# Another order of a pair's score tiles, and the first pair's last tile directly in front of the sums

## The chip, the cores and the metric

The kernel runs on one core of a Trainium2 chip. The metric is the device time of the whole launch in microseconds, smaller is better. The engines are named as the profile names them: PE (TensorE, matmuls) and PEld (its weight loads), DVE (VectorE), ACT (ScalarE), POOL (GpSimd), SP (the queue that issues most DMAs).

## The reference

The input is `x` of 2048 tokens by 448 features. It is normalised (layer norm), and the output is `x` plus attention of the normalised input plus a gated feed-forward layer (FFN) of it:

```python
x = A_x
xn = _layernorm(x, axis=-1)
return x + _A_ref(xn, ...) + _B_ref(xn, ...)
# attention: 16 heads of 28, four segments s of L = 512 tokens
logits = jnp.einsum("bhqd,bhkd->bhqk", qs, ks) * scale + mask      # causal, within the segment
a_dot = jnp.einsum("bhqk,bhkd->bhqd", _softmax(logits, axis=-1), vs)
o = g * a_mem + (1.0 - g) * a_dot          # a_mem: recall from a running memory of earlier segments
# FFN
h = _sigmoid(g) * u                        # g, u: xn times w_gate, w_up (448 x 1792)
return jnp.einsum("bsf,fd->bsd", h, w_down)
```

## The kernel before

A first part (up to about 160 us) normalises, makes queries, keys and values, and does the memory recall. The second part, in which the change lies, runs the FFN and the attention interleaved. The orders of PE and SP are those of the code (`MANUAL`); the orders of ACT, DVE and POOL are chosen by the framework's scheduler, which puts the instructions of both parts into one queue for each engine.

The FFN is a generator. For each of 4 token blocks and each pair of hidden strips it issues runs of 11 matmuls of 512 columns into a bank `pgu` (L247) and, later, runs of six matmuls of 448 columns into `pd` (L173), which DVE adds to `acc` (L174). Between, ACT and DVE make the gated value (`sg`, `hh`, L255 to L259).

The attention is a second generator, of 16 units (counted from 0 here: four segments by four groups of four heads), two pairs of heads each. A unit has 14 slots, and `SLOT` says what stands in each: 0 or 1 is the next step of that pair, 2 the sums of the unit before. The outer loop at the end of the kernel takes a slot from the attention whenever the FFN has gone far enough, so that the slots are spread evenly between the FFN's runs.

A pair's first five steps are its score tiles (`scores`). One tile fills one bank `st` (tag "s", two banks in turn) with keys on the partitions: a head's first key block against 512 queries; its second and fourth blocks, 384 and 128 columns; or both heads' third block, 256 columns twice. Each tile is copied by ACT to `w` (L616 or L619), POOL masks the diagonal blocks (L627), and DVE takes the maximum (L629 over 1024 columns of a head when both of its own tiles are there, L633 over the 512 of the shared tile). A bank can be written again when ACT has copied the tile before the last. After the fifth tile a pair has five more steps (`PARTS`, one at each later slot): a chain of small maxima on DVE and copies on POOL (L643 to L653), a transpose that spreads the maximum (`mb`, L656), and three steps of a subtraction on DVE (L666) and an exponential on ACT (L667). With its last score tile a pair also hands SP the loads of `qk` for the same pair of the next unit (L595); slot 7 hands it the load of `vv` (L679).

The sums (`finish`) are 32 matmul records of 32-column weights, four side by side, from the exponentials and the values into `pa` (L687); DVE then transposes, scales and transposes back (L690, L135, L136, L693).

Of the kernel before, what the change touches and what calls it, by code (L numbers as in the profile page):

```python
# [16 lines left out]
P = 128  # L17
# [5 lines left out]
L = 512  # L23
# [12 lines left out]
LEAD, TAIL = 15, 53  # L36


SLOT = (0, 0, 0, None, 0, 0, None, 2, 1, 1, 1, None, 1, 1)

PARTS = 5

# [1 line left out]
HW = 1280  # L44
# [17 lines left out]
def kernel(  # L62
# [11 lines left out]
    V, A, G, T = nc.vector, nc.scalar, nc.gpsimd, nc.tensor  # L74
# [40 lines left out]
    def bank(name, tag):  # L115
        return ps.tile([P, L], F32, name=name, tag=tag, bufs=banks[tag])
# [159 lines left out]
    with tc.tile_pool(name="front", bufs=2) as sb, tc.manual_schedule(engines=FRONT):  # L276
# [227 lines left out]
        for b in range(NB):  # L504
# [24 lines left out]
            for k, c in enumerate((3, 4, 5, 6, 0, 1, 2) if last else range(7)):  # L529
# [34 lines left out]
                n = k - 1 if b == 0 else k + 1  # L564
# [18 lines left out]
    class Pair:  # L583
# [19 lines left out]
        def scores(self):  # L603

            self.w = sb.tile([P, 2 * HW], F32, name="w", bufs=3)
            w3 = self.w.rearrange("p (h n) -> p h n", h=2)
            mx = sb.tile([P, 80], F32, name="mx", bufs=2)
            for n in range(5):
                st = bank("st", "s")
                for h, kb in (((n // 2, 0),), ((n // 2, 1), (n // 2, 3)))[n % 2] if n < 4 else ((0, 2), (1, 2)):  # L610
                    at = KB[kb] % L + (256 * h if kb == 2 else 0)
                    T.matmul(st[:, at:at + L - kb * P], self.qk[:KS, 1, h, kb * P:(kb + 1) * P],  # L612
                             self.qk[:KS, 0, h, kb * P:], start=True, stop=True)
                if n < 4:
                    w = self.w[:, HW * (n // 2) + L * (n % 2):][:, :L]
                    A.activation(w, st, AF.Copy)  # L616
                else:
                    w = w3[:, :, 2 * L:]
                    A.activation(w, st.rearrange("p (h n) -> p h n", h=2), AF.Copy)  # L619

                if n % 2 == 0 and n < 4:
                    d = w[:, :P]
                    pattern = [[1, P]]
                else:
                    d = w.rearrange("p (a n) -> p a n", n=P)[:, 0:4:3, :] if n < 4 else w[:, :, :P]
                    pattern = [[0, 2], [1, P]]
                G.affine_select(d, d, pattern=pattern, base=0, channel_multiplier=-1, compare_op=ALU.is_ge, fill=MASK)  # L627
                if n in (1, 3):
                    V.tensor_reduce(mx[:, 16 * (n - 1):16 * (n + 1)],  # L629
                                    w3[:, n // 2, :2 * L].rearrange("p (b n) -> p b n", n=32),  # L630
                                    axis=mybir.AxisListType.X, op=ALU.max, apply_transpose=True)
                if n == 4:
                    V.tensor_reduce(mx[:, 64:80].rearrange("p (h b) -> p h b", h=2),  # L633
                                    w.rearrange("p h (b n) -> p h b n", n=32),
                                    axis=mybir.AxisListType.X, op=ALU.max, apply_transpose=True)
                yield
            yield from self.weights(mx)
# [60 lines left out]
    units = [Unit(u, pairs[2 * u:2 * u + 2]) for u in range(NB * NG)]  # L698

    def attention():  # L700
        for n in range(2):
            pairs[n].load()
        units[0].load_values()
        yield
        run, behind, fin = {}, [], None
        for u in range(len(units) + 1):
            for n in range(2):
                run[n] = pairs[2 * u + n].scores() if u < len(units) else iter(())
            for k, which in enumerate(SLOT):
                if u == len(units):  # L710

                    if k > 9:
                        break
                    which = ((None,) * 8 + (2, None))[k]
                if behind:
                    next(behind.pop(0))
                if fin:
                    next(fin)
                    fin = None
                if which is not None and which < 2 and u < len(units):  # L720
                    next(run[which])
                    n = 2 * u + which + 2
                    if which not in SLOT[k + 1:]:
                        behind += [run[which]] * PARTS
                        if n < len(pairs):
                            pairs[n].load()
                        else:
                            load_sums(n - len(pairs))
                if which == 2 and u > 0:
                    fin = units[u - 1].finish()  # L730
                    next(fin)
                    if u < len(units):
                        units[u].load_values()
                yield
# [3 lines left out]
    def load_sums(b):  # L738

        if b < 2:  # L740
            sums[b] = sb.tile([P, HG, L], F32, name="sums", tag="qk2", bufs=2)
        else:
            sums[b] = sums[b - 2]
        o3 = od[b].rearrange("(h c) n -> h c n", c=32)
        for m in range(8):
            a, c = m % 2, 4 * min(m, 6)
            nc.sync.dma_start(sums[b][64 * a:64 * a + 64, m // 2, :], o3[:, c:c + 4, :])
# [32 lines left out]

    N_OUT = 1 + NB * NT * 3 + 12
    steps = attention()
    n_att = len(units) * len(SLOT) + 10
    done = 0
    with tc.manual_schedule(engines=MANUAL):
        next(steps)
        k = sum(FILLS) + 6
# [46 lines left out]
```

## Time and profile before

| | us |
|---|---|
| median of 3 runs (lowest, highest) | 687.41 (687.20, 687.65) |
| the profiled execution | 687.43 |
| its span, first to last instruction | 685.7 |
| PE busy in the span | 679.6 |
| DVE busy | 566.7 |
| ACT busy | 341.6 |
| POOL busy | 147.6 |

The granted TensorE clock is 1.000 over the span. The profile's rows name an engine, a line of the code, an operation and what it writes and reads; behind the bar stand busy time, the mean of one in ns, and the idle time of the engine just before with what ended it. In the order of time, "x11" merges instructions of one line that follow each other, with the shape of the first of them.

### The profile page before, as it was taken

To read this page: it belongs to the slowest core of one execution; us is meant where nothing else is said; L and a number is where in the kernel's file an instruction comes from. 1 tells how busy PE (TensorE), PEld (TensorE's weight loads), DVE (VectorE), ACT (ScalarE), POOL (GpSimd) and SP (SyncE) were. 2 spreads that over 40 slices of the span, in tenths; PEclk is the share of its full clock that TensorE was granted. 3 is DMA by queue.
4 is the path that set the end of the run, shared out by engine and by line. 5 is a ranking of instruction groups with operands and counts; after the bars stand their busy time and mean duration, and the time that the engine had idled before them with its cause. 6 is when DMAs were issued, how large, how long until landed. Compare 5 with 4: busy or idle time off the path is not lost.

```text
span 685.7 us, 10450 instructions
## 1 busy us (share of the span) xinstructions
PE 679.6 (99%) x3594; PEld 565.5 (82%) x3594; DVE 566.7 (83%) x994; ACT 341.6 (50%) x563; POOL 147.6 (22%) x349
## 2 busy tenths in 40 slices
PE   8999999999999999999999999999999999999997
PEld 7898878778878787887878778787887878778897
DVE  6765695767789998988998889988998899889863
ACT  4837555343554455544556446455643465446220
POOL 3500010101223232222232222232321323212000
PEclk9999999999999999999999999999999999999999
DMA  7446556697242333243324243324342423423342
GB/s 268 179 153 233 204 207 244 246 337 179 71 95 78 94 87 86 58 127 83 85 58 112 58 127 70 99 57 117 82 102 69 97 56 86 95 78 91 93 155 107
DMA packets 45796, 84.37 MB, mean 123 GB/s; under 512 B 6320, under 2 KB 20400, under 8 KB 45232
## 3 DMA queue, kind: packets, MB, share of 16 engines
q1 hardware_dynamic: 42736, 76.37, 36.4%
q0 software_dynamic: 3008, 7.34, 5.2%
q8 instruction: 28, 0.46, 0.3%
q14 instruction: 24, 0.20, 0.1%
HBM read 51.05 MB, written 32.64 MB: 122 GB/s over the span
## 4 chain that ended last, share of the span: by engine, by line
PE 97%; DMA 1%; DVE 1%; SPq 0%; issue 0%; ACT 0%; ACTq 0%
PE pgu L247 41%; PE pd L173 20%; PE pp L355 10%; PE st L612 6%; PE pa L687 5%; PE po L771 5%; PE pv L335 5%; PE pmm L383 2%; PE n L401 2%; DMA acc<-in_x 1%; PE pt L95 1%; PE pk L375 1%; DMA vv<-vd 0%; DVE stats L294 0%; DVE acc L775 0%
## 5 line engine op out<-in xcount | busy, mean ns | idle before, releaser
L247 PE MATMUL pgu<-xs,wgu 128*128 128x512 f32 x1232 | 303.6, 393 | 0.0
L247 PEld LDWEIGHTS pgu<-xs,wgu 128*128 128x128 f32 x1232 | 228.2, 188 | 46.9 <-issue 2.4
L173 PE MATMUL pd<-wdn,hh 128*128 128x448 f32 x672 | 155.9, 367 | 0.0
L173 PEld LDWEIGHTS pd<-wdn,hh 128*128 128x128 f32 x672 | 122.4, 188 | 12.0 <-issue 0.8
L627 POOL TENSOR_SCALAR_AFFINE_SELECT w<-w 128x256 f32<-128x256 f32 (+1 forms) x160 | 80.3, 505 | 240.9 <-ACT w L616 192.4
L667 ACT ACTIVATE w<-w 128x1024 f32<-128x1024 f32 (+1 forms) x96 | 87.4, 916 | 88.4 <-DVE w L666 87.9
L666 DVE TENSOR_TENSOR w<-w,mb 128x1024 f32<-128x1024 f32 (+1 forms) x96 | 98.6, 1035 | 0.2
L616 ACT ACTIVATE w<-st 128x512 f32<-128x512 f32 x128 | 74.7, 591 | 43.2 <-PE st L612 42.9
L629 DVE TRANSPOSE_TENSOR_REDUCE mx<-w 128x32 f32<-128x1024 f32 x64 | 78.8, 1231 | 14.8 <-POOL w L627 14.7
L355 PE MATMUL pp<-xs,wqk 128*128 128x512 f32 x308 | 77.7, 401 | 0.0
L174 DVE TENSOR_TENSOR acc<-pd,acc 128x448 f32<-128x448 f32 x112 | 67.2, 600 | 1.1 <-PE pd L173 1.1
L355 PEld LDWEIGHTS pp<-xs,wqk 128*128 128x128 f32 x308 | 56.8, 188 | 13.4 <-issue 2.4
L612 PE MATMUL st<-qk 84*128 84x128 f32 (+3 forms) x256 | 62.3, 313 | 0.1
L258 ACT ACTIVATE hh<-sg 128x512 fp32r<-128x512 f32 x56 | 35.2, 628 | 53.4 <-DVE sg L256 42.2
L612 PEld LDWEIGHTS st<-qk 84*128 84x128 f32 x256 | 47.7, 189 | 7.5 <-ACT w L616 0.7
L255 ACT ACTIVATE sg<-pgu 128x512 f32<-128x512 f32 x56 | 33.1, 592 | 36.2 <-PE pgu L247 36.2
L656 DVE STREAM_TRANSPOSE mb<-top 128x1024 f32<-128x1024 f32 x32 | 39.7, 1242 | 12.6 <-POOL top L653 12.3
L362 DVE TENSOR_TENSOR qk<-pp,qk 128x512 fp32r<-128x512 f32 x28 | 19.3, 689 | 29.8 <-ACT e L360 23.7
L259 DVE SCALAR_TENSOR_TENSOR hh<-sg,hh 128x512 fp32r<-128x512 f32 x56 | 38.9, 694 | 2.8 <-ACT hh L258 2.4
L335 PE MATMUL pv<-wv,xs 128*128 128x448 f32 x176 | 39.6, 376 | 0.4 <-DVE xs L102 0.3
L256 DVE SCALAR_TENSOR_TENSOR sg<-sg,pgu 128x512 f32<-128x512 f32 x56 | 37.3, 667 | 1.7 <-PE pgu L247 1.5
L687 PE MATMUL pa<-w,vv 128*32 128x128 f32 (+3 forms) x512 | 37.9, 436 | 0.0
(100 smaller groups left out, 639.5 us busy)
## 6 DMA issues: line engine op xcount, KB each, us to landing
qk<-qd SPq DMA_DIRECT2D x192, 112.0 KB
qd<-qk SPq DMA_DIRECT2D x28, 512.0 KB
raw<-in_w_ffn SPq DMA_DIRECT2D x14, 512.0 KB
vd<-vst SPq DMA_DIRECT2D x4, 1024.0 KB
vv<-vd SPq DMA_DIRECT2D x16, 256.0 KB
od<-w POOLq DMA_DIRECT2D x16, 256.0 KB, 3.9
sums<-od SPq DMA_DIRECT2D x32, 128.0 KB
out<-acc SPq DMA_DIRECT2D x16, 224.0 KB
```

The costliest lines, as they stand in the source:

```text
L173: T.matmul(pd[:, :D], l, r, start=n == 0, stop=n == len(mms) - 1)
L174: V.tensor_add(acc[b][:, t, :], pd[:, :D], acc[b][:, t, :])
L247: T.matmul(dst, wgu[f][:, w, side * P:(side + 1) * P], xs[b][:, a, :], start=n == 0, stop=n == len(TERMS) - 1)
L335: T.matmul(pv[:, :D], xs[b][:, a, t * P:(t + 1) * P], wv[w], start=n == 0, stop=n == len(TERMS) - 1)
L355: T.matmul(pp, wqk[c][:, w, :], xs[b][:, a, :], start=n == 0, stop=n == len(TERMS) - 1)
L612: T.matmul(st[:, at:at + L - kb * P], self.qk[:KS, 1, h, kb * P:(kb + 1) * P], self.qk[:KS, 0, h, kb * P:], start=True, stop=True)
L616: A.activation(w, st, AF.Copy)
L627: G.affine_select(d, d, pattern=pattern, base=0, channel_multiplier=-1, compare_op=ALU.is_ge, fill=MASK)
L629: V.tensor_reduce(mx[:, 16 * (n - 1):16 * (n + 1)], w3[:, n // 2, :2 * L].rearrange("p (b n) -> p b n", n=32), axis=mybir.AxisListType.X, ...
L666: V.tensor_sub(w, w, m)
L667: A.activation(w, w, AF.Exp, scale=SCALE)
L687: T.matmul(pa[32 * j:32 * j + 32, kb * P:], self.vv[:, kb, 32 * j:32 * j + 32], self.pairs[j // 2].block(j % 2, kb), start=kb == 0, stop=k ...
```

## The change

The order of a pair's five tiles changes. Before: first head 512, first head 384 and 128, second head 512, second head 384 and 128, both heads 256. After: first head 512, second head 512, both heads 256, first head 384 and 128, second head 384 and 128. The reductions move with the tiles: the one of 512 columns comes third instead of last.

The slots change for the first pair: its tiles stood in slots 0, 1, 2, 4, 5 and now stand in 0, 1, 3, 5, 7. A slot can now hold two things, and slot 7 holds the first pair's last tile and, behind it, the sums. Everything that follows a pair's last tile (the five later steps and the load of `qk`) moves from slot 5 to slot 7 with it. The second pair stays in slots 8, 9, 10, 12, 13.

```diff
-SLOT = (0, 0, 0, None, 0, 0, None, 2, 1, 1, 1, None, 1, 1)
+SLOT = ((0,), (0,), (), (0,), (), (0,), (), (0, 2), (1,), (1,), (1,), (), (1,), (1,))
...
             for n in range(5):
                 st = bank("st", "s")
-                for h, kb in (((n // 2, 0),), ((n // 2, 1), (n // 2, 3)))[n % 2] if n < 4 else ((0, 2), (1, 2)):
+                h = n % 2 if n < 2 else n - 3
+                for h, kb in (((h, 0),), ((0, 2), (1, 2)), ((h, 1), (h, 3)))[(0, 0, 1, 2, 2)[n]]:
...
-                if n in (1, 3):
-                    V.tensor_reduce(mx[:, 16 * (n - 1):16 * (n + 1)],
-                                    w3[:, n // 2, :2 * L].rearrange("p (b n) -> p b n", n=32),
+                if n > 2:
+                    V.tensor_reduce(mx[:, 32 * h:32 * h + 32],
+                                    w3[:, h, :2 * L].rearrange("p (b n) -> p b n", n=32),
...
-                if n == 4:
+                if n == 2:
...
-                if which is not None and which < 2 and u < len(units):
+                for which in now:
+                    if which == 2:
+                        continue
                     next(run[which])
                     n = 2 * u + which + 2
-                    if which not in SLOT[k + 1:]:
+                    if not any(which in later for later in SLOT[k + 1:]):
                         behind += [run[which]] * PARTS
...
-                if which == 2 and u > 0:
+                if 2 in now and u > 0:
                     fin = units[u - 1].finish()
                     next(fin)
```

Lines from 612 on move by one in the changed kernel (L612 becomes L613 and so on, by three at the end). Names carry a buffer number; `xs2` and such are the four token blocks.

On PE, the stretch in front of the sums of unit 5's slot 7. Before:

```order
L247 MATMUL pgu_3285<-xs2_67,wgu_2492 128x512 x11
L612 MATMUL st_3299<-qk2_3017 128x384
L612 MATMUL st_3299<-qk2_3017 128x128
L612 MATMUL st_3307<-qk2_3017 128x256 x2
L173 MATMUL pd_3322<-wdn_2627,hh_2974 128x448 x3
L173 MATMUL pd_3322<-wdn_2918,hh_3084 128x448 x3
L247 MATMUL pgu_3341<-xs2_67,wgu_2492 128x512 x11
L687 MATMUL pa_3361<-w_2910,vv_3063 32x512 x2
```

The same stretch now:

```order
L247 MATMUL pgu_3285<-xs2_67,wgu_2486 128x512 x11
L613 MATMUL st_3299<-qk2_3025 128x384
L613 MATMUL st_3299<-qk2_3025 128x128
L173 MATMUL pd_3307<-wdn_2625,hh_2966 128x448 x3
L173 MATMUL pd_3307<-wdn_2918,hh_3071 128x448 x3
L247 MATMUL pgu_3315<-xs2_67,wgu_2486 128x512 x11
L613 MATMUL st_3333<-qk2_3025 128x384
L613 MATMUL st_3333<-qk2_3025 128x128
L688 MATMUL pa_3348<-w_2910,vv_3050 32x512 x2
```

The pair's last tile went from in front of a run of six to directly in front of the sums; the runs around it are the same.

On ACT, in unit 14: `w_6007` is its first pair; `w_6194` (before) and `w_6190` (now) are its second pair. Before:

```order
L667 ACTIVATE w_6007<-w_6007 128x2x512
L255 ACTIVATE sg_6232<-pgu_6175 128x512
L616 ACTIVATE w_6194<-st_6196 128x512
L667 ACTIVATE w_6007<-w_6007 128x2x2x256
L616 ACTIVATE w_6194<-st_6212 128x512
L667 ACTIVATE w_6007<-w_6007 128x2x2x128
L616 ACTIVATE w_6194<-st_6240 128x512
L258 ACTIVATE hh_6235<-sg_6232 128x512
L255 ACTIVATE sg_6331<-pgu_6254 128x512
L616 ACTIVATE w_6194<-st_6266 128x512
```

Now:

```order
L617 ACTIVATE w_6190<-st_6192 128x512
L617 ACTIVATE w_6190<-st_6208 128x512
L668 ACTIVATE w_6007<-w_6007 128x2x512
L258 ACTIVATE hh_6229<-sg_6226 128x512
L620 ACTIVATE w_6190<-st_6234 128x2x256
L668 ACTIVATE w_6007<-w_6007 128x2x2x256
L255 ACTIVATE sg_6331<-pgu_6252 128x512
L668 ACTIVATE w_6007<-w_6007 128x2x2x128
L617 ACTIVATE w_6190<-st_6266 128x512
L617 ACTIVATE w_6190<-st_6274 128x512
L617 ACTIVATE w_6308<-st_6310 128x512
```

The first pair's three exponentials moved behind the second pair's first two copies, and the third of them stands in front of the copy of its fourth tile (`st_6266`); the bank of that tile is the next unit's first (`st_6310`).

On DVE, the same unit: `mb` is the first pair's spread maximum, `w_6007` its scores. Before:

```order
L656 STREAM_TRANSPOSE mb_6153<-top_6138 128x1024
L666 TENSOR_TENSOR w_6007<-w_6007,mb_6153 128x2x512
L690 STREAM_TRANSPOSE w_5883<-pa_6155 128x512
L666 TENSOR_TENSOR w_6007<-w_6007,mb_6153 128x2x2x256
L135 RECIPROCAL rc_6189<-w_5883 128x16
L666 TENSOR_TENSOR w_6007<-w_6007,mb_6153 128x2x2x128
L136 SCALAR_TENSOR_TENSOR w_5883<-w_5883,gate_n_77,rc_6189 128x16x28
```

Now, where the sums' four instructions and the chain of maxima stand in front of the first of these rows:

```order
L657 STREAM_TRANSPOSE mb_6206<-top_6178 128x1024
L174 TENSOR_TENSOR acc3_72<-pd_6198,acc3_72 128x448
L667 TENSOR_TENSOR w_6007<-w_6007,mb_6206 128x2x512
L256 SCALAR_TENSOR_TENSOR sg_6226<-sg_6226,pgu_6214 128x512
L667 TENSOR_TENSOR w_6007<-w_6007,mb_6206 128x2x2x256
L259 SCALAR_TENSOR_TENSOR hh_6229<-sg_6226,hh_6229 128x512
L174 TENSOR_TENSOR acc3_72<-pd_6244,acc3_72 128x448
L634 TENSOR_REDUCE mx_6191<-w_6190 128x16
L667 TENSOR_TENSOR w_6007<-w_6007,mb_6206 128x2x2x128
```

The subtractions moved from around the sums' transpose to behind all of the sums' work on DVE, with FFN instructions and a reduction of the second pair between them.

More of the change, by code (lines that the diff above doesn't have):

```diff
@@ L613, in scores @@
                              self.qk[:KS, 0, h, kb * P:], start=True, stop=True)
-                if n < 4:
-                    w = self.w[:, HW * (n // 2) + L * (n % 2):][:, :L]
+                if n != 2:
+                    w = self.w[:, HW * h + L * (n // 2 > 0):][:, :L]
                     A.activation(w, st, AF.Copy)
@@ L619, in scores @@
                     A.activation(w, st.rearrange("p (h n) -> p h n", h=2), AF.Copy)
-                if n % 2 == 0 and n < 4:
+                if n < 2:
                     d = w[:, :P]
@@ L624, in scores @@
                 else:
-                    d = w.rearrange("p (a n) -> p a n", n=P)[:, 0:4:3, :] if n < 4 else w[:, :, :P]
+                    d = w.rearrange("p (a n) -> p a n", n=P)[:, 0:4:3, :] if n > 2 else w[:, :, :P]
                     pattern = [[0, 2], [1, P]]
                 G.affine_select(d, d, pattern=pattern, base=0, channel_multiplier=-1, compare_op=ALU.is_ge, fill=MASK)
-                if n in (1, 3):
-                    V.tensor_reduce(mx[:, 16 * (n - 1):16 * (n + 1)],
-                                    w3[:, n // 2, :2 * L].rearrange("p (b n) -> p b n", n=32),
+                if n > 2:
+                    V.tensor_reduce(mx[:, 32 * h:32 * h + 32],
+                                    w3[:, h, :2 * L].rearrange("p (b n) -> p b n", n=32),
                                     axis=mybir.AxisListType.X, op=ALU.max, apply_transpose=True)
-                if n == 4:
+                if n == 2:
                     V.tensor_reduce(mx[:, 64:80].rearrange("p (h b) -> p h b", h=2),
@@ L708, in attention @@
                 run[n] = pairs[2 * u + n].scores() if u < len(units) else iter(())
-            for k, which in enumerate(SLOT):
+            for k, now in enumerate(SLOT):
                 if u == len(units):
@@ L713, in attention @@
                         break
-                    which = ((None,) * 8 + (2, None))[k]
+                    now = (2,) if k == 8 else ()
                 if behind:
```

## The prediction, made blind

> **What bounds the kernel now.** I read the profile's page first (busy times, then the chain of work that ended last), then who waited for the scores, then the order of time on TensorE around one unit.
>
> ```profile
> PE 679.6 (99%) x3594; PEld 565.5 (82%) x3594; DVE 566.7 (83%) x994; ACT 341.6 (50%) x563; POOL 147.6 (22%) x349
> PE 97%; DMA 1%; DVE 1%; SPq 0%; issue 0%; ACT 0%; ACTq 0%
>   PEld st L612: 0.7, 3
> ```
>
> TensorE is busy 99% of the 685.7 us span and makes up 97% of the chain. The third row is from the list of who waited for the score tiles: in the whole kernel the load of a score matmul waited three times, 0.7 us together, for a score bank that ScalarE had not yet copied out. So the end is set by the sum of TensorE's own steps, in the order in which the program issues them, plus those few waits. An edit that only reorders can act in two ways: a matmul becomes dearer or cheaper by its neighbours, or a wait appears or goes.
>
> The profiled execution took 687.43 us, 1.7 us more than its span; the median of the runs is 687.41, so the sum below is made against 687.4 without a correction.
>
> **What a step costs on TensorE.** The order of time around unit 5, merged; the first column is the start, the second the length (which holds the drain of the last matmul, so I use differences of starts).
>
> ```profile
> 299.71 1.38 PE L173 MATMUL pd<-wdn,hh 128*128 128x448 f32 x6
> 300.93 2.65 PE L247 MATMUL pgu<-xs,wgu 128*128 128x512 f32 x11
> 303.42 0.40 PE L612 MATMUL st<-qk 84*128 84x384 f32 x2
> 303.65 1.42 PE L173 MATMUL pd<-wdn,hh 128*128 128x448 f32 x6
> 304.91 0.40 PE L612 MATMUL st<-qk 84*128 84x256 f32 x2
> 305.15 2.69 PE L247 MATMUL pgu<-xs,wgu 128*128 128x512 f32 x11
> 307.68 0.40 PE L612 MATMUL st<-qk 84*128 84x512 f32 x1
> 307.91 1.38 PE L173 MATMUL pd<-wdn,hh 128*128 128x448 f32 x6
> 309.13 0.40 PE L612 MATMUL st<-qk 84*128 84x384 f32 x2
> ...
> 315.89 0.68 PE L612 MATMUL st<-qk 84*128 84x384 f32 x4
> 316.41 1.37 PE L173 MATMUL pd<-wdn,hh 128*128 128x448 f32 x6
> 317.62 2.65 PE L247 MATMUL pgu<-xs,wgu 128*128 128x512 f32 x11
> 320.20 2.36 PE L687 MATMUL pa<-w,vv 128*32 128x512 f32 x32
> 322.49 1.47 PE L173 MATMUL pd<-wdn,hh 128*128 128x448 f32 x6
> 323.80 0.40 PE L612 MATMUL st<-qk 84*128 84x512 f32 x1
> ```
>
> Eleven 512-column matmuls take 300.93 to 303.42, 2.49 us (0.227 each); six of 448 columns take 1.21 (316.41 to 317.62). A 512-column score tile takes 0.23 to 0.24. A tile of 384 and 128 columns takes 303.42 to 303.65 and lets the six after it take 1.26 instead of 1.21: 0.28 together. A tile of 256 twice takes 0.24, and 0.04 in the run after it. Two tiles in one place (x4, 315.89 to 316.41) take 0.52, the sum of the two kinds.
>
> The hand-over to the sums is where a neighbour matters. The run at 317.62 needs 2.58 us until the sums start, 0.09 more than 2.49; after the sums six matmuls take 1.31 instead of 1.21, another 0.10.
>
> ```profile
> 320.20 0.16 PEld L687 LDWEIGHTS pa<-w,vv 128*32 128x32 f32 x8 [0.35 <-issue]
> L247 PEld LDWEIGHTS pgu<-xs,wgu 128*128 128x128 f32 x1232 | 228.2, 188 | 46.9 <-issue 2.4
> L612 PE MATMUL st<-qk 84*128 84x512 f32 x64 | 25.9, 405 | 0.1
> L612 PE MATMUL st<-qk 84*128 84x128 f32 x64 | 14.2, 222 | 0.0
> ```
>
> The sums' first weight load comes after 0.35 us in which no load ran, and no semaphore ended that time ("issue"); it begins 0.32 us after the last 512-column matmul (317.62 plus ten times 0.227 is 319.89). Elsewhere the 188 ns loads run under the matmul ahead, since 0.227 per pair leaves no room beside it. So this load, of another width, seems to be held until the matmul ahead has streamed, plus some 0.1 us.
>
> **The change, part by part.**
>
> 1. *The 384 and 128 columns of the first pair stand directly in front of the sums, in 15 units* (the first unit has no sums, and the last sums have no scores ahead). A 128-column matmul ends its stream 0.17 us sooner than one of 512 columns (384 columns at 0.227/512 each; by the recorded lengths, 405 against 222 ns, 0.18). Held until that end, the load would begin 0.32 - 0.17 = 0.15 us after the 128-column matmul. That matmul's own share is 0.11 in any place (0.28 less 384 columns at 0.227/512 = 0.17). The hand-over then costs 0.15 - 0.11 = 0.04 instead of 0.09. Times 15: -0.7 us. Ends: if all of the 0.09 goes, -1.35; if the hand-over does not depend on the columns, 0. A loss, the load beginning a fixed time after the matmul ahead has started, would cost 0.12 each, but one place speaks against it: behind six of 448 columns (unit 14) the sums come 1.31 after the run's start, 0.10 over 1.21, and a fixed start would leave 0.12. These rows, at 0.01 us each, let a slope between 0.3 and 0.45 ns a column stand, which is 0 to 0.05 saved; I take the upper part, since a stream's own pace is 0.44.
>
> ```profile
> 581.93 1.38 PE L173 MATMUL pd<-wdn,hh 128*128 128x448 f32 x6
> 583.24 2.36 PE L687 MATMUL pa<-w,vv 128*32 128x512 f32 x32
> ...
> 598.09 0.40 PE L612 MATMUL st<-qk 84*128 84x512 f32 x1
> ```
>
> 2. *All other places of the scores.* The same 64 tiles of 512, 64 of 384 and 128, 32 of twice 256 columns stand between the same runs, elsewhere; by the costs above this is within 0.05 us over the kernel: 0.
>
> 3. *The three waits for a score bank (0.7 us of load idle; some of it lies under the matmul ahead, so 0.5 on the path).* ScalarE's order has the first pair's exponentials, which wait for VectorE, ahead of the second pair's first copies. The new order has these copies ahead of nearly all of them: -0.5. Ends: 0 and -0.7.
>
> 4. *The first pair's chain (maximum, transpose, three subtractions, exponentials) begins two slots later and now shares VectorE with the sums' four instructions.* In unit 14 the copy of the second pair's fourth tile stands behind the third exponential, and the next unit's first score needs that bank. What VectorE has to do from the end of the sums to the third subtraction, by these rows:
>
> ```profile
> L666 DVE TENSOR_TENSOR w<-w,mb 128x1024 f32<-128x1024 f32 x64 | 76.8, 1205 | 0.2
> L174 DVE TENSOR_TENSOR acc<-pd,acc 128x448 f32<-128x448 f32 x112 | 67.2, 600 | 1.1 <-PE pd L173 1.1
> L629 DVE TRANSPOSE_TENSOR_REDUCE mx<-w 128x32 f32<-128x1024 f32 x64 | 78.8, 1231 | 14.8 <-POOL w L627 14.7
> L633 DVE TRANSPOSE_TENSOR_REDUCE mx<-w 128x16 f32<-128x512 f32 x32 | 22.2, 695 | 2.2 <-POOL w L627 2.2
> L656 DVE STREAM_TRANSPOSE mb<-top 128x1024 f32<-128x1024 f32 x32 | 39.7, 1242 | 12.6 <-POOL top L653 12.3
> L259 DVE SCALAR_TENSOR_TENSOR hh<-sg,hh 128x512 fp32r<-128x512 f32 x56 | 38.9, 694 | 2.8 <-ACT hh L258 2.4
> L649 DVE TENSOR_TENSOR mx<-mx,up 64x32 f32<-64x32 f32 x32 | 5.8, 181 | 7.6 <-POOL up L648 7.4
> L667 ACT ACTIVATE w<-w 128x512 f32<-128x512 f32 x32 | 20.1, 627 | 9.6 <-DVE w L666 9.6
> L616 ACT ACTIVATE w<-st 128x512 f32<-128x512 f32 x128 | 74.7, 591 | 43.2 <-PE st L612 42.9
> ```
>
> Two subtractions of 1024 (2.41), two additions (1.20), one transpose of 1024 (1.24), seven instructions of about 512 columns (0.69 each, 4.86), six small ones (0.18 each, 1.09) and waits for POOL's copies inside the chain (about 0.8; the rows show 12.3 in 32 and 7.4 in 32, and the other copy of a maximum waits alike): 11.6 us. The sums take 2.36 from 583.24, so the third exponential (0.63) and then the copy (0.59) end 15.2 us after the sums' start; the next unit's first score stands at 598.09, 14.85 after it. It waits 0.35: +0.4. The other units have the same chain with less FFN work in it, or the copy ahead of the third exponential (seven of the first fifteen): 0. Ends: 0, and the slower rival below.
>
> 5. *Covered.* The load of the next unit's first pair is issued two slots later, by SP, ahead of the same load of values. Rows: issue at 316.61, DMA quiet again in the third window, first use at 336.26. Two slots are about 4 us, and some 10 of the 20 remain. If they were gone, each us late would be one on TensorE. The copies, masks (POOL) and reductions are the same in number and size; VectorE's FFN instructions stand mostly 0.5 to 3 us of work earlier in its order (the rows ahead of each, by the durations above), since reductions of 1.23 us moved behind them.
>
> ```profile
> 316.61 1.61 SPq L595 DMA_DIRECT2D qk<-qd  x4
> ...
> 322.00:324.00 2.00, 2.00 (x23) 1.63 (x16) 1.22 (x5) 0.60 (x1) 0.73 (x4) 1.00 0.01 3
> ...
> 336.26 0.40 PE L612 MATMUL st<-qk 84*128 84x512 f32 x1
> ```
>
> Sum: -0.7 + 0 - 0.5 + 0.4 = -0.8, so 687.4 - 0.8 = 686.6 us.
>
> **The rivals.**
>
> *The whole hand-over goes.* If the 0.09 is time that a 128-column matmul's own 0.11 covers, 15 x 0.09 = 1.35 go, the waits go (0.5) and unit 14 does not wait: 687.4 - 1.85 = 685.6. For it: the 0.35 of idle loads is named only "issue". Against it: it needs the load to begin within 0.11 us of a 128-column matmul, where 0.32 was seen behind 512.
>
> *The hand-over stays.* A slope of 0.3 ns a column leaves 0.09 at each: -0.5 + 0.4, 687.3. [...]
>
> *Slower: the score banks wait for the late exponentials.* In eight units (3, 4, 5, 7, 8, 10, 12, 14) the copy of the fourth tile stands behind the first pair's third exponential. VectorE is at 83% of the span, and if it comes to the third subtraction 1 us later than counted, unit 14 waits 1.4 us; with 0.3 in each of the other seven that is 3.5, and 687.4 - 1.2 + 3.5 = 689.7. It decides from 0.3 us in each of the eight on. For it: three such waits exist now. Against it: between the second pair's chain VectorE now has a reduction of 0.70 us in place of one of 1.23, and the other units' chains have less in them than unit 14's.
>
> **How the numbers follow.** About 0.2% (1.4 us) is what a measurement of this kernel can tell from no change. Forecast 0.50 (its own range 686.1 to 687.2), whole hand-over gone 0.14, hand-over stays 0.18, late exponentials 0.16 with everything else that makes a wait. Faster than 686.0: the second case and a little of the first, 0.18. Slower than 688.8: most of the last, 0.15. Same 0.67. The range leaves out the best end of the second case and the worst half of the last: 685.6 to 688.4.
>
> **What would show it.** Step 1: from the start of the pair of 384 and 128 columns to the start of the sums, 0.32 us (0.37 if the hand-over stays, 0.28 if it goes). Step 2: TensorE's other differences of starts as above. Steps 3 and 4: the list of who waited for the score tiles, with the load's waits at or under 0.7 us, one of them at the first score of the last unit. Wrong would be: loads of scores waiting in many units, or an idle TensorE before the sums that a semaphore ends.

## The result, and the profile after

The changed kernel takes 695.33 us (median of 4, 695.24 to 696.48); the kernel before, on the same chip, 687.5 (median of 4). The ratio is 1.0119, 95% interval 1.0106 to 1.0131: slower by 1.2%, some 7.8 us, where 0.8 us less was forecast. The profiled execution has a span of 693.7 us, 8.0 more than before, at a granted clock of 1.000.

The page's busy times and its chain of work that ended last:

```profile
PE 682.1 (98%) x3594; PEld 566.8 (82%) x3594; DVE 568.6 (82%) x994; ACT 340.7 (49%) x563; POOL 144.6 (21%) x349
...
PE 33%; DVE 28%; issue 26%; POOL 9%; ACT 3%; POOLq 0%; DMA 0%; ACTq 0%; DVEq 0%
```

The engines do nearly the same work as before, in the same number of instructions, and TensorE is still busy for 98% of the span. But the chain, of which TensorE was 97%, is now TensorE for 33%, VectorE for 28%, GpSimd for 9% and ScalarE for 3% of its length; another 26% is "issue", time in which the engine waited for nothing that the profile shows. The list of who waited for the score tiles (us in total, times) and the list of TensorE's waits (us in total, times, longest) say where TensorE stands still:

```profile
  PEld st L613: 9.9, 13
  PE st L613: 5.6, 9
```

```profile
PE st L613 <- ACT w L617: 4.8, 8, 1.4
...
PE st L613 <- ACT w L620: 0.9, 1, 0.9
PE pa L688 <- ACT w L668: 0.5, 1, 0.5
```

The loads of the score matmuls waited 13 times for 9.9 us, where it was 3 times for 0.7. These rows overlap each other and the matmul ahead, so the loss is counted from differences of starts, each against the usual distance of the same neighbours. Gaps ahead of score tiles, with the 0.1 us by which the next matmul is late after each, come to 8.5 us (0.5 before). Four more entries complete the sum. The sums of unit 3, with a wait for an exponential inside them, last 3.40 us from first to last start instead of 2.09 (+1.3). The hand-overs to the sums are cheaper by 0.8, and the last sums by 0.1. The first sums begin 0.4 earlier (202.8 against 203.2), before any of this plays a part. 8.0 + 1.3 - 0.8 - 0.1 - 0.4 is the 8.0 us.

The hand-over itself, in the order of time around unit 5's slot 7:

```profile
318.69 2.65 PE L247 MATMUL pgu<-xs,wgu 128*128 128x512 f32 x11
321.19 0.40 PE L613 MATMUL st<-qk 84*128 84x384 f32 x2
321.51 2.36 PE L688 MATMUL pa<-w,vv 128*32 128x512 f32 x32
323.80 1.47 PE L173 MATMUL pd<-wdn,hh 128*128 128x448 f32 x6
```

From the start of the pair of 384 and 128 columns to the sums it is 0.32 us, as forecast; the run ahead takes 2.50 instead of 2.58.

What went wrong is seen in one unit. Unit 14, from the sums to the next unit's first score, all engines in the order of time:

```profile
589.01 2.36 PE L688 MATMUL pa<-w,vv 128*32 128x512 f32 x32
...
590.41 0.63 ACT L258 ACTIVATE hh<-sg 128x512 fp32r<-128x512 f32 x1 [1.56 <-DVE sg L256]
...
590.95 0.58 ACT L617 ACTIVATE w<-st 128x512 f32<-128x512 f32 x1
...
592.06 1.25 DVE L630 TRANSPOSE_TENSOR_REDUCE mx<-w 128x32 f32<-128x1024 f32 x1 [0.30 <-POOL w L628]
593.23 0.67 DVE L691 STREAM_TRANSPOSE w<-pa 128x512 f32<-128x512 f32 x1
...
594.95 0.71 DVE L694 STREAM_TRANSPOSE w<-w 128x512 f32<-128x512 f32 x1
...
595.96 0.87 POOL L695 DMA_DIRECT2D od<-w  x1 [0.62 <-DVE mx L650]
596.88 0.20 POOL L651 COPY up<-mx 32x32 f32<-32x32 f32 x1
597.11 0.18 DVE L652 TENSOR_TENSOR top<-mx,up 32x32 f32<-32x32 f32 x1 [1.38 <-POOL up L651]
...
597.63 0.29 POOL L628 TENSOR_SCALAR_AFFINE_SELECT w<-w 128x128 f32<-128x128 f32 x1
...
598.23 1.25 DVE L657 STREAM_TRANSPOSE mb<-top 128x1024 f32<-128x1024 f32 x1 [0.93 <-POOL top L654]
...
604.58 0.65 DVE L667 TENSOR_TENSOR w<-w,mb 128x512 f32<-128x512 f32 x1
605.32 0.63 ACT L668 ACTIVATE w<-w 128x512 f32<-128x512 f32 x1 [0.62 <-DVE w L667]
605.86 1.07 ACT L617 ACTIVATE w<-st 128x512 f32<-128x512 f32 x2
...
606.49 0.50 PE L613 MATMUL st<-qk 84*128 84x512 f32 x1 [1.40 <-ACT w L617]
```

Read it from the bottom. The next unit's first score (606.49) waited for a copy, the copy stood behind the third exponential, and that waited for the third subtraction (604.58). The subtraction was late because the spread of the maximum (598.23) was late, and that in part because GpSimd had the sums' output DMA (595.96, 0.87 us) in its queue between two copies of the chain: the maximum behind the second copy (597.11) waited 1.38 us. In the 0.93 us that the spread itself waited stands a mask (597.63, 0.29 us) between the chain's last two copies. Further up, the last reduction (592.06) waited for a copy that ScalarE did only at 590.95, behind `hh`.

### The profile page after: what moved, and what is told of

It reads as the page before. It is cut to its first block, busy times and chain, and to the rows that moved or that the text cites. A ratio compares the mean times of both kernels' runs of the same rounds, so it can differ in the third digit from the quotient of the medians.

```text
span 693.7 us, 10506 instructions
## 1 busy us (share of the span) xinstructions
PE 682.1 (98%) x3594; PEld 566.8 (82%) x3594; DVE 568.6 (82%) x994; ACT 340.7 (49%) x563; POOL 144.6 (21%) x349
## 4 chain that ended last, share of the span: by engine, by line
PE 33%; DVE 28%; issue 26%; POOL 9%; ACT 3%; POOLq 0%; DMA 0%; ACTq 0%; DVEq 0%
PE pp L355 8%; DVE mx L630 7%; PE pgu L247 6%; POOL w L628 5%; PE po L774 5%; PE pv L335 4%; PE pd L173 4%; DVE w L667 4%; DVE acc L174 3%; DVE sg L256 2%; DVE hh L259 2%; PE pmm L383 2%; DVE w L691 1%; PE pa L688 1%; DVE mb L657 1%
## 5 line engine op out<-in xcount | busy, mean ns | idle before, releaser
L628 POOL TENSOR_SCALAR_AFFINE_SELECT w<-w 128x256 f32<-128x256 f32 (+1 forms) x160 | 74.2, 465 | 255.1 <-ACT w L617 204.9
L613 PE MATMUL st<-qk 84*128 84x128 f32 (+3 forms) x256 | 63.9, 315 | 5.7 <-ACT w L617 4.8
L613 PEld LDWEIGHTS st<-qk 84*128 84x128 f32 x256 | 47.9, 189 | 16.7 <-ACT w L617 8.8
```

## The experiments

The first theory (D): in unit 14 above, GpSimd's copy at 596.88 began only behind the DMA (595.96, 0.87 us), and now that the first pair's chain runs at the same time as the sums' work on VectorE, the sums' output DMA falls between the chain's copies. In GpSimd's order it stands there in none of the 15 units before and in 8 after (units 1, 4, 6, 8, 9, 11, 13, 14). The rival (L): the chain is two slots later, and that alone uses up the room before the next score. Further rivals are named with the runs. The kernel before ran beside every group of runs; its medians were 687.24 to 687.3. The changed kernel did not, so a difference from its 695.33 is uncertain by some 0.2 us more.

**One part of the change at a time.** e1 has the new order of tiles in the old slots, e2 the old order in the new slots.

```diff
 e1, against the changed kernel
-SLOT = ((0,), (0,), (), (0,), (), (0,), (), (0, 2), (1,), (1,), (1,), (), (1,), (1,))
+SLOT = ((0,), (0,), (0,), (), (0,), (0,), (), (2,), (1,), (1,), (1,), (), (1,), (1,))
 e2, against the changed kernel (the copies' places, masks and reductions follow, as before)
-                h = n % 2 if n < 2 else n - 3
-                for h, kb in (((h, 0),), ((0, 2), (1, 2)), ((h, 1), (h, 3)))[(0, 0, 1, 2, 2)[n]]:
+                for h, kb in (((n // 2, 0),), ((n // 2, 1), (n // 2, 3)))[n % 2] if n < 4 else ((0, 2), (1, 2)):
```

> The new order of the tiles in the old slots (first pair in 0, 1, 2, 4, 5), so its chain begins where it did before, and the sums follow a run of the FFN. Theory S (the slots: the chain that begins two slots later makes ScalarE's copies, and with them the score banks, late): the 8 us are gone, 686.9 to 688.0, and the load's waits for score banks are under 1.5 us. Theory O (the order: two reductions of 1024 columns now end a pair's scores, 1.23 us instead of 0.70 in the last place): most of the loss stays, 692 to 695.

> The old order of the tiles in the new slots, so the tile of twice 256 columns stands in front of the sums. Theory S: most of the loss stays, 692 to 696, with the waits at the next unit's first score. Theory O: 687 to 689. The hand-over to the sums is read besides: a 256-column matmul ends its stream 0.11 us sooner than one of 512, so by the held load the hand-over costs about what it did before less 0.1, within 0.02.

e1 took 690.15 us (ratio 1.0042, 1.0025 to 1.0059), e2 690.2 (1.0043, 1.0028 to 1.0058). Each part alone costs 2.9 us, and both together 7.8: neither is the cause by itself, and together they cost 2 us more than their sum. The kernel of e1 was run once more for the profile that is read here (e7):

> The kernel of e1_order_only once more, for a profile at full clock: where its 2.9 us over the kernel before come from. If the new order of the tiles alone makes the first pair's chain late (two reductions of 1.23 us instead of one of 1.23 and one of 0.70 behind the last tile), the score tiles wait some 2 to 3 us in all, behind exponentials on ScalarE, at the first tiles of some units, and VectorE's waits for POOL's copies are no longer than before. If it is something else (dearer score tiles in pairs on TensorE), the waits for score banks stay under 1 us and the runs around the scores are longer.

It took 690.32 us. Who waited for the score tiles, first in e7, then in e2:

```profile
  PEld st L613: 2.2, 5
```

```profile
  PEld st L612: 3.4, 6
```

And the sums of unit 3 on TensorE's timeline, before, in e7 and in e2:

```profile
290.29 2.36 PE L687 MATMUL pa<-w,vv 128*32 128x512 f32 x32
```

```profile
290.41 3.20 PE L688 MATMUL pa<-w,vv 128*32 128x512 f32 x32
```

```profile
290.50 2.82 PE L687 MATMUL pa<-w,vv 128*32 128x512 f32 x32
```

In e7 the gaps at score tiles come to 2.3 us (0.5 before), 0.8 of which is an FFN run behind a score that waits for `sg`, and two of the sums wait, 0.84 us in unit 3 and 0.4 more than before in the last one. In e2 the gaps are 2.9 us, and two sums wait 0.45 and 0.66. So the expected score waits of e7 were there in part, but some two fifths of the loss is in the sums, which I had not listed. The hand-over that e2 was to show came as expected: the sums start 0.21 us after the start of the second matmul of 256 columns, 0.11 sooner than behind 512.

What differs between e2 and the changed kernel can be counted. On GpSimd, the sums' output DMA stands inside the first pair's chain in one unit of e2 and in none of e7, against eight of the changed kernel: it takes both parts of the change to put it there, which fits that together they cost more than their sum. On VectorE, a reduction of 1.23 us stands between the first pair's spread maximum and its third subtraction in 15 units of e2, in none of the changed kernel, which has one of 0.70 there in 12.

**Another bank for the one tile that waits** (e3): each unit's first score tile is written to a bank of another tag.

```diff
-                st = bank("st", "s")
+                st = bank("st", "p" if n == 0 and self.first else "s")
```

> The changed kernel, but the first pair's first tile of each unit takes a bank of the ring that the FFN's second gate matmuls use, so that it no longer waits for the copy of the tile two before it. Theory B (the loss is on TensorE only through the score banks): the waits at that tile go, 687 to 690. Rival L (the whole loop of both pairs is too long for its 28.8 us, banks or not): the wait comes back at the next tile or at the sums, 693 to 695.

It took 693.2 us (1.0093, 1.0076 to 1.011), 2.1 less than the changed kernel. Its TensorE waits:

```profile
PE st L614 <- ACT w L621: 2.0, 3, 1.5
...
PE st L614 <- ACT w L618: 1.5, 2, 0.8
PE pa L689 <- ACT w L669: 1.0, 1, 1.0
```

With the first tile out of the way the others wait, and the sums of unit 3 last 3.95 us, as the rival said: the bank is where the lateness shows, and only a part of the loss depends on it.

**The output DMA behind the chain** (e4): GpSimd may start the sums' DMA only after the last copy of the first pair's chain.

```diff
-            G.tensor_copy(top[64:128], top[0:64])
+            self.topped = G.tensor_copy(top[64:128], top[0:64]).ins
...
-            nc.gpsimd.dma_start(od[s][P * i:P * (i + 1)], oc, accum_op=ALU.add if s > 0 else ALU.bypass)
+            after = ...  # topped of the next unit's first pair
+            with (tc.issue_after(after) if after is not None else ExitStack()):
+                nc.gpsimd.dma_start(od[s][P * i:P * (i + 1)], oc, accum_op=ALU.add if s > 0 else ALU.bypass)
```

> The changed kernel, but on POOL the sums' output DMA (0.87 us) is held behind the four copies of the first pair's chain of maxima; in eight of the units it stands between them now. Theory D (that DMA in the chain is the cause): the third exponential comes about 1 us sooner in these units, the waits fall to a third, 688 to 690. Theory S alone: the chain is late by the late start, of which this is the smaller part, 692 to 695.

It took 688.76 us (1.0022, 1.0013 to 1.0032): of the 7.8 us, 6.6 are gone. The gaps at score tiles fall from 8.5 to 2.1 us, and the loads that waited from 9.9 us to this:

```profile
  PEld st L614: 2.7, 5
```

But the scheduler also orders ScalarE and VectorE anew around the held DMA, so this alone does not tell the DMA from the exponentials' places. The next two do.

**ScalarE's order held, with and without the DMA's place** (e8, e9). In both, each of the first pair's exponentials stands behind the copy of the second pair's tile of the same slot; e9 has e4's edge besides.

```diff
 e8, against the changed kernel
-                    A.activation(w, st, AF.Copy)
+                    self.copied.append(A.activation(w, st, AF.Copy).ins)
...
+            ahead = pairs[self.n + 1].copied if self.n % 2 == 0 else ()
...
-                A.activation(w, w, AF.Exp, scale=SCALE)
+                with (tc.issue_after(ahead[-1]) if ahead else ExitStack()):
+                    A.activation(w, w, AF.Exp, scale=SCALE)
 and in a slot: scores first, then the later step, then the rest of the sums
```

> The changed kernel, with ScalarE's order alone held: each of the first pair's three exponentials stands behind the copy of the second pair's score tile that PE issues in the same slot (and the order inside a slot is scores, chain, rest of the sums). The sums' output DMA stays where the scheduler puts it on POOL. Theory (a late chain costs only because exponentials stand ahead of copies): nearly all of the 8.5 us of waits go, 687 to 688. Rival (the copies themselves come late because VectorE and POOL delay everything, or the sums wait): 691 or more.

> e8_copies_first with the sums' output DMA behind the first pair's chain on POOL as in e4_output_behind_chain. Theory: 686.6 to 687.0, that is the prediction's hand-over gain of 0.7 with all waits gone. Rival (2 us of waits that neither edge removes remain): 688.8 as e4_output_behind_chain.

e8 took 693.98 us (1.0097, 1.0082 to 1.0112), e9 687.13 (0.9998, 0.9988 to 1.0007). Score loads that waited, and VectorE's longest kinds of wait inside the chain (us in total, times, longest), in e8:

```profile
  PEld st L614: 8.8, 11
```

```profile
DVE mb L658 <- POOL top L655: 15.2, 21, 2.0
DVE top L653 <- POOL up L652: 6.9, 16, 1.4
```

and in e9:

```profile
  PEld st L615: 1.0, 3
```

```profile
DVE mb L659 <- POOL top L656: 8.4, 17, 0.7
DVE top L654 <- POOL up L653: 5.0, 16, 0.4
```

The theory that I had for e8 fell: the exponentials' place ahead of the copies costs some 1.35 us of the 7.8 and no more. Held or not, a copy comes too late when the exponentials are late, for `hh`, `sg` and the first two exponentials still stand in the queue. The edge on the DMA is worth 6.85 us between e8 and e9; in e8 the DMA stands inside 8 chains, in e9 in none. Not all that moves with it is the DMA, because the scheduler follows the held instruction. On VectorE the order of the chain's small maxima and of the sums' four instructions is the same in e8 and e9 in every unit but 14, where the chain now begins ahead of the sums' work; and the masks inside the first pairs' chains go from 14 to 10. No run moves the DMA with all else held. In e9's unit 14 the spread of the maximum starts 6.8 us after the sums' start (583.09), against 9.2 in the changed kernel, and the DMA comes behind it:

```profile
589.88 1.25 DVE L659 STREAM_TRANSPOSE mb<-top 128x1024 f32<-128x1024 f32 x1
...
590.24 0.87 POOL L702 DMA_DIRECT2D od<-w  x1 [0.39 <-DVE w L699]
```

The waits are where it stands, too. Of the gaps at score tiles in the changed kernel, 7.6 us in 11 places without the late matmul after each, 6.5 us follow the first pairs of units 6, 8, 9, 11, 13 and 14, six of the eight; the rest follow units 3 and 7. In e9 the gaps are as small as before, 0.56 us, and what keeps it from its 686.6 is the sums of unit 3, 3.06 us instead of 2.09.

**The same cost in every unit** (e14): e8, with the chain's second copy held behind the DMA. The DMA needs the sums' last transpose on VectorE, so the chain waits for that too.

```diff
-            G.tensor_copy(up[0:32], m0[32:64])
+            with (tc.issue_after(self.sent) if self.sent is not None else ExitStack()):
+                G.tensor_copy(up[0:32], m0[32:64])
...
+            sent = nc.gpsimd.dma_start(od[s][P * i:P * (i + 1)], oc, accum_op=ALU.add if s > 0 else ALU.bypass).ins
```

> e8_copies_first (693.98) with the suspected cost put into every unit: POOL's second copy in the first pair's chain is held behind the sums' output DMA, so that the DMA stands inside the chain in 14 units instead of 8. Theory (the DMA inside the chain makes every following step late, and TensorE pays for it in each unit): e9_both, which has none inside, took 687.13; 8 inside cost 6.85, 0.86 each; 14 inside give 687.1 + 14 x 0.86 = 699, or 697 if some of the six new places have room. Rival (the eight were places without room, the others have it): 694 to 695.

It took 699.55 us (1.0179, 1.0165 to 1.0193). VectorE's waits inside the chain:

```profile
DVE top L654 <- POOL up L653: 20.6, 27, 1.5
DVE mb L659 <- POOL top L656: 11.9, 21, 0.9
```

The size fits: none inside 687.1, 8 inside 694.0, 14 inside 699.6. That it comes so close to 699 is partly luck, and the even price of 0.86 each does not hold. The gaps at score tiles come to 7.8 us without the late matmul after each, in units 3, 7, 8, 9, 10, 12 and 15 only; three of the sums wait, 0.9, 2.3 and 1.1 us; and behind one wait of 2.1 us the next eleven matmuls take 4.0 us instead of 2.5, some 1.5 us more (see the last section). Lateness is paid where the next unit happens to have no room.

**The wait that is left in e9** (e10, e12, e13, and e11 as a control). e10 gives the second pair its old order of tiles in e9, e12 does the same in the changed kernel with nothing held. e11 is the kernel before with ScalarE's order held as in e8.

```diff
 e10 and e12
-            for n in range(5):
+            for n in (range(5), (0, 3, 1, 4, 2))[self.n % 2]:
```

> e9_both, with the second pair's five tiles in their old order (first head 512, first head 384 and 128, second head 512, second head 384 and 128, both heads 256) and the first pair's in the new. In e9_both the scores wait as little as before, but the sums of unit 3 last 3.06 us from first to last matmul instead of 2.09, waiting for an exponential of the second pair, in whose chain two reductions of 1.23 us now stand behind the last tile. Theory (that wait comes from the second pair's tile order): it goes, 687.13 less 0.97 = 686.2, about 1 us under the kernel before. Rival (it comes from the slots): 687.1.

> The changed kernel with nothing held, the second pair's tiles in the old order. The slots and the sums' output DMA inside the chain stay. Theory (the DMA inside the chain costs most, the second pair's order some): 691 to 693.5. If the second pair's order is the whole cause: 688 or less. If it has no part: 695.

> A control: the kernel before, old order and old slots, with ScalarE's order held as in e8_copies_first and the rest of the sums handed out behind the scores of slot 8. No hand-over changes. Theory (a gain of e10_both_mixed is the hand-over's): 687.0 to 687.4, at best the 0.5 us of the three waits less. Rival (the held order is what is faster): 686.3 or less.

e10 took 690.92 us (1.0053, 1.0041 to 1.0066), e12 697.13 (1.0143, 1.0129 to 1.0157), e11 689.03 (1.0026, 1.0016 to 1.0035). All three are worse than expected. In e10 unit 3's sums do wait less (2.62 us instead of 3.06), but the score tiles wait again, and VectorE's timeline of unit 14 suggests why:

```profile
  PEld st L615: 6.2, 9
```

```profile
593.42 1.25 DVE L659 STREAM_TRANSPOSE mb<-top 128x1024 f32<-128x1024 f32 x1
594.70 1.37 DVE L670 TENSOR_TENSOR w<-w,mb 128x1024 f32<-128x1024 f32 x1
595.99 0.61 DVE L174 TENSOR_TENSOR acc<-pd,acc 128x448 f32<-128x448 f32 x1
596.52 1.23 DVE L632 TRANSPOSE_TENSOR_REDUCE mx<-w 128x32 f32<-128x1024 f32 x1
597.68 1.18 DVE L670 TENSOR_TENSOR w<-w,mb 128x1024 f32<-128x1024 f32 x1
```

The second pair's reduction of 1.23 us stands between the first pair's first two subtractions. In 14 units of e10 and 13 of e12 one stands somewhere between the spread of the maximum and the third subtraction. With the new order it is one of 0.70, in 12 units. So the new order of the second pair seems to be a help to a late first pair; this is argued from the orders. It fits what e2 has, whose chains hold such a reduction in all 15 units. For its size, compare e9 with e10 (3.8 us): of the 1.8 us between the changed kernel and e12, most is the slower TensorE behind one wait that the last section shows. e11, without late slots, has nearly no score waits (0.3 us) but sums that wait: 1.16 us more in unit 3, 0.57 in unit 7, 0.2 in the last. The kernel before has little room there as well.

e13 takes e9 and moves the first pair's third tile to slot 4, its reduction behind the second pair's third subtraction, and the second pair's later steps ahead of the scores again.

```diff
-SLOT = ((0,), (0,), (), (0,), (), (0,), (), (0, 2), (1,), (1,), (1,), (), (1,), (1,))
+SLOT = ((0,), (0,), (), (), (0,), (0,), (), (0, 2), (1,), (1,), (1,), (), (1,), (1,))
...
+                    less = pairs[self.n - 1].less if self.n % 2 == 0 and self.n else None
+                    with (tc.issue_after(less) if less is not None else ExitStack()):
```

> e9_both with three further edits against the one wait left, that of unit 3's sums for the second pair's last exponential (0.97 us): the first pair's third tile (both heads 256) in slot 4 instead of 3, its reduction on VectorE behind the third subtraction of the last unit's second pair (0.70 us earlier for that subtraction), and the second pair's later steps ahead of the scores in a slot again. Theory (the new places cost nothing but waits): 686.2 to 686.6, the first kernel faster than before, by the hand-over's 0.7 to 0.8. Rival (a late chain has no room anywhere, the wait turns up at another tile): 687 to 688.

It took 687.21 us (0.9999, 0.999 to 1.0008). Unit 3's sums no longer wait; the score tiles wait 1.0 us more:

```profile
290.64 2.37 PE L695 MATMUL pa<-w,vv 128*32 128x512 f32 x32
```

```profile
  PEld st L615: 2.2, 5
```

The rival holds: the wait moved. No version beat the kernel before by more than a measurement can tell.

## Why the prediction was wrong

*Step 1, the hand-over, was right.* 0.32 us from the pair of 384 and 128 columns to the sums was forecast and measured. Over all places, the pair and the sums together cost 51 ns less (between a run of 512 and one of 448 columns) or 62 ns less (the other way round) than the two apart; 0.05 was forecast, -0.7 us in all, and -0.8 came. The dependence on the columns holds too: from the start of the matmul ahead to the sums it is 0.32 us behind 512 columns, 0.30 behind 448, 0.21 behind 256 (e2) and 0.15 behind 128. That is 0.17 us for 384 columns, 0.44 ns a column, as the prediction took it; that the load is held until the matmul ahead has streamed fits this, but no row shows it by itself. Both rivals on the hand-over fall: it neither goes whole (0.28 us) nor stays (0.37).

*Step 2, the other places of the scores, was right* at 0: single tiles between runs cost the same to 0.01 us after as before.

*Step 3, the three waits that go, was wrong.* It looked at ScalarE's order alone, where copies now stand ahead of exponentials. The waits rose from 0.7 to 9.9 us, 13 of them, the sign of being wrong that the prediction itself had named, since the exponentials that remain ahead of copies are later than before by more than the order gives back. e8 shows how little the order is worth: with all held, some 1.35 us.

*Step 4, the late chain, had the right mechanism and failed in its size*: with step 3, the score waits were to change by -0.1 us, and they grew by 8.0. Its count for unit 14 was 15.2 us from the sums' start to the end of the copy; the trace has 17.4 (589.01 to 606.4, when the first of the two copies has ended). Three terms of the count were off:
- VectorE was taken to begin the sums' work when the sums end (591.4). It began at 593.23, 1.9 us later, behind a reduction that waited for a mask and a copy behind `hh`.
- The waits for GpSimd inside the chain were taken at 0.8 us, from the rows of before. The two longest were 1.38, behind the sums' output DMA, and 0.93, with a mask between the copies. The step counted the sums' four instructions on VectorE and not their fifth, on GpSimd, although the chain was moved right past it. This is the failed step, a term of the chain's waits that was left out: taking the DMA out of the chains gave back 6.6 us (e4) and 6.85 (from e8 to e9), with what the scheduler moves along. In unit 14 alone the DMA is the smaller part, about 1.0 of the 2.2 us that were missing (1.38 against at most 0.4 for the same wait in e9). Its weight in the whole is that it stands in eight units, where step 4 worked out one.
- By difference, the rest of the listed work took some 1.1 us less than counted.

*"The other units: 0"* failed with it. Waits turned up in 11 places, from unit 4 to unit 15. The slower rival (late exponentials, 689.7, chance 0.16) was the right case in kind, at a third of the size, and its eight units were read from ScalarE's order. Four of the eight (3, 7, 8, 14) have the wait at the next unit's first score; the other waits are at places that the order of one engine does not show.

*Step 5, covered,* held for the loads: what ended the waits of score matmuls was ScalarE's copies in every row, never a load. But the masks, taken as unchanged "in number and size", were not unchanged in place: they stand inside the chains 20 times instead of 6.

*Not foreseen at all* were waits of the sums for the second pair's exponentials (1.3 us in unit 3). The second pair kept its slots and was dropped from the argument, but its two reductions of 1.23 us now both follow its last tiles. That is a part of it: e7, with the old slots, has 0.84 us of this wait, and e10, with the second pair's old order, still has 0.53.

A smaller reading: the four chances (0.50, 0.14, 0.18, 0.16) add up to 0.98.

## What to carry to other kernels

When a chain of small steps is moved in time, list every instruction that every queue will then hold beside it, above all on a queue that also issues DMAs; waits taken from the rows of the old place are no price for the new one. When one engine is 99% busy, as here, the room is in the slack of the others, and it differs from unit to unit: some 1 us in a chain reached TensorE after six of eight units and not after the other two. So a delay in many units is not hidden because it is hidden in the one that was counted. And an order that is worse for one chain can be better for its neighbour: the two parts of this change cost 2.9 us each alone, and undoing half of one in e9 cost 3.8 (e10).

## What the runs showed of the hardware

In two profiles a wait on TensorE cost more than its own length. In e12 one score waited 3.2 us for its bank, and the eleven matmuls behind it took 4.0 us instead of 2.5. The timeline, and busy times of the engines by stretch with the granted clock (the column behind POOL's):

```profile
606.11 0.50 PE L614 MATMUL st<-qk 84*128 84x512 f32 x1 [3.17 <-ACT w L618]
606.44 4.21 PE L247 MATMUL pgu<-xs,wgu 128*128 128x512 f32 x11
610.45 0.50 PE L614 MATMUL st<-qk 84*128 84x512 f32 x1
```

```profile
590.00:602.50 12.50, 12.50 (x70) 10.64 (x61) 9.72 (x18) 3.63 (x7) 3.05 (x9) 1.00 0.43 80
602.60:606.10 3.50, 0.34 (x2) 0.00 (x0) 3.11 (x5) 3.33 (x6) 0.00 (x0) 1.00 0.77 196
606.10:610.50 4.40, 4.39 (x13) 3.43 (x14) 2.96 (x7) 1.44 (x3) 1.51 (x5) 0.63 0.01 1
```

The granted clock is 0.63 over the stretch behind the wait, and the eleven matmuls there take 0.365 us each (606.44 to 610.45) instead of 0.227: 1.5 us more on top of the wait. In e14's profile it was the same behind a wait of 2.1 us (4.0 us for the eleven, a clock of 0.63 from 521.9 to 526.5), while behind 1.4 us in the profile of the changed kernel's unit 14 they took 2.54 us. The length alone seems not to decide: two of e14's four executions have a granted clock of 0.997 and 0.998 and take 700.0 and 700.4 us, the other two have 1.000 and take 699.1 and 699.0; and one of the changed kernel's four has 0.997 and takes 1.1 to 1.2 us longer than the rest. That these drops come behind the same waits is not shown, for only one execution of a kernel has a profile. What decides no run here tells.

A DMA in GpSimd's queue held up the copy behind it: in the changed kernel's unit 14 `up` (596.88) had its input at 595.7 and stood 1.2 us, through the 0.87 us of the DMA ahead of it.
